# Accumulating e K Vᵀ per head in the forward of a decode block's gradient, so that the backward need not read K

## The chip, the cores and the metric

The kernel runs on one core of a Trainium2 chip. The metric is device time in microseconds (us), the median of several executions; one further execution under the profiler gives the trace.

Engines are called as in the profile: PE is TensorE's matmuls, PEld its weight loads, DVE is VectorE, ACT is ScalarE, POOL is GpSimd, SP is SyncE (here it only issues transfers).

## The reference

It is one token going through an attention block with a cache and an MLP block, with the gradient of the whole. Cut to what matters:

```python
D, F, Hq, Sk, Dh = 640, 1536, 32, 8192, 192           # one token
mod = (silu(c) @ w_mod).reshape(1, 6, 1, -1)           # sa, ca, ga, sb, cb, gb
h = layernorm(x) * (1 + ca) + sa
q = (h @ wq) as 32 heads of 192
p = softmax(q . K * Dh**-0.5)                          # K, V: (32, 8192, 192) bf16
o = p @ V
x = x + ga * (o @ wo)
h = layernorm(x) * (1 + cb) + sb
x = x + gb * MLP(h)                                    # w3, w4, tanh gelu
# outputs: x, and the gradients of x, K, V, wq, wo, w3, w4, c, w_mod
```

For one query the gradients of the attention are, for each head and with `c = do . o`:

```
dP_j = V_j . do        dS_j = p_j (dP_j - c)
dV_j = p_j do          dK_j = dS_j q          dq = sum_j dS_j K_j
```

K and V are 100.7 MB each (32 x 8192 x 192 x 2 bytes), and so are dK and dV. Nearly all the time goes into moving these four and into work over their elements. Notice that only the last of the formulas, dq, needs K in the backward. With `e_j` for the unnormalised softmax weight and Z for their sum,

```
dq = ( (sum_j e_j K_j V_j^T) do  -  c sum_j e_j K_j ) / Z
```

and the two sums over j do not depend on the backward at all.

## The kernel before

Each head's 8192 rows lie as 128 partitions times 64 rows, loaded in halves of 32 rows (6144 elements on each partition; P = 128, J = 64, JH = 32, DH = 192). Here are the parts that the change and the argument touch.

The forward of a head: dot products with K on VectorE (8 of 32 rows are summed by ScalarE), softmax, then p V on TensorE with one-column weights.

```python
def fwd_stage_a(h):
    for t in range(2):
        nc.sync.dma_start(out=K_sb, in_=K_hd[h][:, js, :])
        nc.sync.dma_start(out=V_sb, in_=V_hd[h][:, js, :])
        nc.vector.tensor_tensor(out=prod, in0=K_sb, in1=qh[:, None, :].to_broadcast([P, JH, DH]), op=ALU.mult)
        for jj in range(JACC_F):
            nc.scalar.activation(out=junk, in_=prod[:, jj, :], func=ACT.Copy, accum_out=S_h[...])
        # ... two halving adds and a reduce_sum for the other rows
def fwd_stage_b(h, S_h, V_halves):
    # ... maximum over the partitions by a transpose, exp into E_all[:, h, :]
    for j in range(J):
        nc.tensor.matmul(o_ps, lhsT=E_all[:, h, j : j + 1], rhs=V_halves[t][:, jj, :], start=(j == 0), stop=(j == J - 1))
```

The backward of a head reads V and K again. dV and dK are made one row of 192 at a time, 15 of 32 rows on ScalarE and 17 on VectorE:

```python
def bwd_stage_a(h):
    for t in range(2):
        nc.sync.dma_start(out=V_sb, in_=V_hd[h][:, js, :])
        nc.sync.dma_start(out=K_sb, in_=K_hd[h][:, js, :])
        nc.vector.tensor_tensor(out=prod, in0=V_sb, in1=doh[:, None, :].to_broadcast([P, JH, DH]), op=ALU.mult)
        # ... two halving adds and a reduce_sum into dP; dS = (dP - c) * P; dS_bf
def bwd_stage_b(h, K_halves, dS_l, dSbf_l):
    for t in range(2):
        for jj in range(JH):
            nc.tensor.matmul(dq_ps, lhsT=dS_bf[:, jj : jj + 1], rhs=K_sb[:, jj, :], start=(j == 0), stop=(j == J - 1))
        for jj in range(JH):
            if jj < JA:            # 15
                nc.scalar.activation(out=dV[:, jj, :], in_=doh, func=ACT.Copy, scale=P_all[:, h, j : j + 1])
                nc.scalar.activation(out=dK[:, jj, :], in_=qh, func=ACT.Copy, scale=dS[:, jj : jj + 1])
            else:
                nc.vector.tensor_scalar(out=dV[:, jj, :], in0=doh, scalar1=P_all[:, h, j : j + 1], scalar2=None, op0=ALU.mult)
                nc.vector.tensor_scalar(out=dK[:, jj, :], in0=qh, scalar1=dS[:, jj : jj + 1], scalar2=None, op0=ALU.mult)
        st_eng.dma_start(out=dV_hd[h][:, js, :], in_=dV)
        st_eng.dma_start(out=dK_hd[h][:, js, :], in_=dK)
```

Everything between the loops (layer norms, MLP and its gradient) works on rows of one partition, 640 or 1536 elements long, which are turned into columns by matmuls and back:

```python
def vecmat(col_bf, nk, W_sb, N, out_row, chunk=512, ...):    # a row = column^T W
    nc.tensor.matmul(ps[0:1, : hi - lo], lhsT=col_bf[:, i : i + 1], rhs=W_sb[:, i, lo:hi], ...)
def row_to_col(row_ap, ncols, out_aps, ...):
    nc.tensor.matmul(ps[:, i : i + 1], lhsT=row_ap[0:1, i * P : (i + 1) * P], rhs=one[0:1, 0:1], ...)
```

The gradient of wo is made between the loops, those of wq and w_mod after the backward, when dq of all heads is there.

## Time and profile before

The median is 1872.15 us in three runs (1871.21 to 1873.1).

| stage | from, to (us) | time | per head |
|---|---|---|---|
| start: mod, q | 0 to 58 | 58 | |
| forward of 32 heads | 58 to 606 | 548 | 16.7 from the fifth head on, 17.1 in the mean |
| middle: MLP and its gradient, do | 606 to 787 | 181 | |
| backward of 32 heads | 787 to 1757 | 970 | about 30 |
| tail: gradients of wq, w_mod, x, c | 1757 to 1871 | 114 | |

These are lines of the page of the kernel before: the busy time of each engine, the packets, and the shares of the chain of waits that ended last.

```profile
PE 767.4 (41%) x5447; PEld 571.7 (31%) x5447; DVE 1490.0 (80%) x3065; ACT 1026.4 (55%) x3391; POOL 101.3 (5%) x180
...
DMA packets 113278, 678.95 MB, mean 363 GB/s; under 512 B 53779, under 2 KB 53782, under 8 KB 63382
...
DMA 44%; DVE 38%; PE 9%; issue 5%; ACT 2%; POOL 1%; DVEq 0%; POOLq 0%; SPq 0%
```

And the table by windows, one line for each of the last four stages. Its columns are the window, its length, the busy time of PE, PEld, DVE, ACT and POOL (with their instructions), the granted clock, the DMA share and GB/s. The DMA share is the mean busy share of the core's 16 DMA engines:

```profile
58.10:606.00 547.90, 281.94 (x2263) 232.07 (x2263) 450.75 (x349) 223.27 (x1181) 2.38 (x1) 0.69 0.95 377
606.00:787.00 181.00, 104.26 (x486) 58.12 (x486) 69.29 (x139) 32.63 (x69) 19.38 (x26) 0.62 0.54 153
787.00:1757.00 970.00, 305.97 (x2342) 240.46 (x2340) 888.07 (x2509) 700.64 (x2040) 68.34 (x128) 0.63 0.99 417
1757.00:1871.00 114.00, 24.94 (x136) 11.36 (x136) 72.03 (x43) 48.41 (x66) 10.10 (x17) 0.58 0.53 212
```

Read them together. In both loops the DMA engines are full or nearly so (0.95 and 0.99), and VectorE is not far behind: 451 of 548 us in the forward, 888 of 970 in the backward. In the other two stages nothing is full: DMA 0.54 and 0.53, VectorE 38% and 63%. Those are chains of short operations that wait for one another. The chain of waits of the backward shows the DMA limit directly. It goes from one V transfer to the product that frees its buffer, to the next V transfer (start, us, what):

```profile
1203.99 26.57 DMA V_sb<-in_A_v_cache_dram
...
1230.59 3.37 DVE bprod L595
```

Three groups of VectorE (count, then busy time and the mean ns of one, then the idle time before it) price the work. A product over 6144 elements takes 3.34 to 3.36 us; a scaled row of 192 takes 0.271 us, so that 17 of them take 4.6 us:

```profile
L629 DVE TENSOR_SCALAR dK<-qs_bc,dS 128x192 bf16<-128x192 bf16 x1088 | 293.9, 271 | 0.0
...
L595 DVE TENSOR_TENSOR bprod<-V_sb,do_bc 128x6144 bf16<-128x6144 bf16 x64 | 215.1, 3361 | 61.3 <-DMA V_sb<-in_A_v_cache_dram 61.3
...
L346 DVE TENSOR_TENSOR prod<-K_sb,qs_bc 128x6144 bf16<-128x6144 bf16 x64 | 213.7, 3340 | 18.0 <-DMA K_sb<-in_A_k_cache_dram 17.9
```

### The profile page before, as it was taken

The page shows a single profiled execution, that of the slowest core. Times are in us where ns is not written, and L with a number is a line of the kernel's source. Part 1 is how long each engine was busy: PE and PEld are TensorE (multiplying, and loading weights), DVE is VectorE, ACT ScalarE, POOL GpSimd, SP SyncE. Part 2 cuts the span into 40 slices and gives each one's busy share as a digit, 9 for nine tenths or more (in the row PEclk, how much of TensorE's full clock was granted, in tenths as well). Part 3 has the DMA queues.
Part 4 walks back from the last instruction along what each step waited for, and adds up shares of the span by engine and source line. Part 5 has one row for each costly group of instructions (what it writes and reads, how often), then busy time and mean ns, then how long its engine had stood idle before and what let it go on. Part 6 is the DMA issues. An engine that isn't in the chain of part 4 may idle for free.

```text
span 1871.0 us, 18774 instructions
## 1 busy us (share of the span) xinstructions
PE 767.4 (41%) x5447; PEld 571.7 (31%) x5447; DVE 1490.0 (80%) x3065; ACT 1026.4 (55%) x3391; POOL 101.3 (5%) x180
## 2 busy tenths in 40 slices
PE   8435554555555755542322324132232313233510
PEld 5234443444444424131222213132221212222300
DVE  1668888888888254399899999999999999999485
ACT  3434444444444211295767777776777777778452
POOL 0000000000000010100000000000000000000010
PEclk8767676777677765665656666565656666566855
DMA  8799999999997426699999999999999999997944
GB/s 341 293 410 397 380 377 382 371 376 380 378 382 287 135 74 170 228 419 429 428 429 430 428 429 430 429 428 429 419 429 408 425 429 430 429 417 312 406 183 158
DMA packets 113278, 678.95 MB, mean 363 GB/s; under 512 B 53779, under 2 KB 53782, under 8 KB 63382
## 3 DMA queue, kind: packets, MB, share of 16 engines
q1 hardware_dynamic: 87590, 440.03, 59.2%
q0 software_dynamic: 25584, 237.71, 30.3%
q8 instruction: 43, 0.70, 0.1%
q14 instruction: 61, 0.50, 0.1%
HBM read 440.01 MB, written 225.91 MB: 356 GB/s over the span
## 4 chain that ended last, share of the span: by engine, by line
DMA 44%; DVE 38%; PE 9%; issue 5%; ACT 2%; POOL 1%; DVEq 0%; POOLq 0%; SPq 0%
DMA V_sb<-in_A_v_cache_dram 38%; DVE prod L346 11%; DVE bprod L595 7%; DVE S_h L355 4%; DMA K_sb<-in_A_k_cache_dram 3%; PE col_ps L188 2%; PE vm_ps L200 2%; DVE dK L629 2%; DVE dV L628 1%; PE vb_ps L121 1%; PE negm_ps L368 1%; DMA out_dram<-dK 1%; DVE dP L601 1%; DMA wmod_sb<-in_w_mod_dram 1%; ACT E_all L372 1%
## 5 line engine op out<-in xcount | busy, mean ns | idle before, releaser
L619 PE MATMUL dq_ps<-K_sb,dS_bf 128*1 128x192 bf16 x2048 | 263.8, 309 | 576.4 <-ACT dS_bf L605 576.4
L626 ACT ACTIVATE dK<-qs_bc,dS 128x192 bf16<-128x192 bf16 x960 | 355.4, 441 | 169.4 <-DMA out_dram<-dK 165.1
L619 PEld LDWEIGHTS <-dS_bf 128*1 128x1 bf16 x2048 | 211.4, 106 | 623.7 <-ACT dS_bf L605 588.2
L625 ACT ACTIVATE dV<-do_bc,P_all 128x192 bf16<-128x192 bf16 x960 | 355.4, 441 | 75.1 <-DMA out_dram<-dV 73.7
L349 ACT ACTIVATE junk<-prod 128x192 bf16<-128x192 bf16 x512 | 178.0, 348 | 215.3 <-DVE prod L346 215.3
L629 DVE TENSOR_SCALAR dK<-qs_bc,dS 128x192 bf16<-128x192 bf16 x1088 | 293.9, 271 | 0.0
L628 DVE TENSOR_SCALAR dV<-do_bc,P_all 128x192 bf16<-128x192 bf16 x1088 | 293.4, 271 | 0.1
L595 DVE TENSOR_TENSOR bprod<-V_sb,do_bc 128x6144 bf16<-128x6144 bf16 x64 | 215.1, 3361 | 61.3 <-DMA V_sb<-in_A_v_cache_dram 61.3
L379 PE MATMUL o_ps<-V_sb,E_all 128*1 128x192 bf16 x2048 | 239.6, 295 | 0.0
L346 DVE TENSOR_TENSOR prod<-K_sb,qs_bc 128x6144 bf16<-128x6144 bf16 x64 | 213.7, 3340 | 18.0 <-DMA K_sb<-in_A_k_cache_dram 17.9
L379 PEld LDWEIGHTS <-E_all 128*1 128x1 bf16 x2048 | 204.5, 102 | 28.2
L349 ACT ACTIVATION_READ_ACCUMULATOR junk<-prod 128x1 f32 x512 | 95.4, 186 | 0.0
L630 POOL DMA_DIRECT2D out_dram<-dV x64 | 34.3, 536 | 874.9 <-DVE dK L629 735.0
L375 DVE RECIPROCAL rinv_all<-tot_ps 1x1 f32<-1x1 f32 x32 | 5.0, 155 | 56.4 <-PE tot_ps L374 56.4
L631 POOL DMA_DIRECT2D out_dram<-dK x64 | 34.1, 533 | 18.2 <-DVE dK L629 17.9
L544 DVE TENSOR_SCALAR dwo_sb<-dao_bc,o_col_f 128x640 bf16<-128x640 bf16 x48 | 15.8, 393 | 24.2 <-DMA out_dram<-dwo_sb 23.1
L384 ACT ACTIVATE o_h<-o_ps,rinv_all 1x192 f32<-1x192 f32 x32 | 13.2, 411 | 37.9 <-PE o_ps L379 37.9
L121 PE MATMUL vb_ps<-woT,dao_col_bf 128*1 128x512 bf16 x60 | 23.0, 524 | 23.3 <-DMA woT<-in_A_wo_dram 23.3
L413 POOL DMA_DIRECT2D w_sb<-in_B_w_dram x1 | 0.9, 892 | 570.9 <-PE vm_ps L200 570.9
L125 ACT CAST do_row_bf<-vb_ps 1x512 bf16<-1x512 f32 x12 | 6.8, 574 | 43.6 <-PE vb_ps L121 43.6
L368 PE MATMUL negm_ps<-negm,ones_row_f 1*128 1x1 f32 x64 | 18.6, 357 | 19.4 <-ACT negm L366 19.4
L368 PEld LDWEIGHTS negm_ps<-negm,ones_row_f 1*128 1x128 f32 x64 | 15.9, 305 | 28.8 <-ACT negm L366 28.8
(893 smaller groups left out, 1259.8 us busy)
## 6 DMA issues: line engine op xcount, KB each, us to landing
K_sb<-in_A_k_cache_dram SPq DMA_DIRECT2D x128, 1536.0 KB, 14.7
V_sb<-in_A_v_cache_dram SPq DMA_DIRECT2D x128, 1536.0 KB, 15.1
out_dram<-dV POOLq DMA_DIRECT2D x64, 1536.0 KB, 14.5
out_dram<-dK POOLq DMA_DIRECT2D x64, 1536.0 KB, 21.3
wq_sb<-in_A_wq_dram SPq DMA_DIRECT2D x1, 7680.0 KB, 33.4
wo_sb<-in_A_wo_dram POOLq DMA_DIRECT2D x1, 7680.0 KB, 69.5
out_dram<-dwo_sb POOLq DMA_DIRECT2D x12, 640.0 KB, 5.0
out_dram<-stg POOLq DMA_DIRECT2D x10, 768.0 KB, 4.3
```

What stands on the lines that cost most here:

```text
L121: nc.tensor.matmul(ps[0:1, : hi - lo], lhsT=col_bf[:, i : i + 1], rhs=W_sb[:, i, lo:hi], start=(i == 0), stop=(i == nk - 1))
L346: nc.vector.tensor_tensor(out=prod, in0=K_sb, in1=qh[:, None, :].to_broadcast([P, JH, DH]), op=ALU.mult)
L349: nc.scalar.activation(out=junk, in_=prod[:, jj, :], func=ACT.Copy, accum_out=S_h[:, t * JH + jj : t * JH + jj + 1])
L355: nc.vector.reduce_sum(out=S_h[:, t * JH + JACC_F : (t + 1) * JH], in_=h2, axis=AX.X)
L368: nc.tensor.matmul(negm_ps, lhsT=ones_row_f[0:1, :], rhs=negm[0:1, 0:1], start=True, stop=True)
L379: nc.tensor.matmul(o_ps, lhsT=E_all[:, h, j : j + 1], rhs=V_halves[t][:, jj, :], start=(j == 0), stop=(j == J - 1))
L595: nc.vector.tensor_tensor(out=prod, in0=V_sb, in1=doh[:, None, :].to_broadcast([P, JH, DH]), op=ALU.mult)
L619: nc.tensor.matmul(dq_ps, lhsT=dS_bf[:, jj : jj + 1], rhs=K_sb[:, jj, :], start=(j == 0), stop=(j == J - 1))
L625: nc.scalar.activation(out=dV[:, jj, :], in_=doh, func=ACT.Copy, scale=P_all[:, h, j : j + 1])
L626: nc.scalar.activation(out=dK[:, jj, :], in_=qh, func=ACT.Copy, scale=dS[:, jj : jj + 1])
L628: nc.vector.tensor_scalar(out=dV[:, jj, :], in0=doh, scalar1=P_all[:, h, j : j + 1], scalar2=None, op0=ALU.mult)
L629: nc.vector.tensor_scalar(out=dK[:, jj, :], in0=qh, scalar1=dS[:, jj : jj + 1], scalar2=None, op0=ALU.mult)
```

## The change

The intent is to take K's second reading (101 MB) out of the backward, to take the rows of one partition out of the middle, and to leave no separate stage for the weight gradients.

- **Forward.** Each K row is scaled by its `e_j` (16 rows at a time: 10 on VectorE, 6 on ScalarE), and TensorE accumulates `(e K)ᵀ [1, V]` over the head: two matmuls with full 128-column weights for each row. V lands in pieces of two rows (768 bytes), between columns of ones that give `sum e K` and Z along with the rest. Four columns of e behind the 192 of K give o.
- **A scalar in four copies.** To multiply a vector by one scalar per row in one `tensor_tensor`, `e_j` is stored four times over. The innermost dimension of every operand then steps by one element, over four elements.
- **Backward.** It reads V alone. dK is one product over 6144 elements; of dV, 18 of 32 rows go to ScalarE one by one and 14 are one product over 2688 elements.
- **Vectors as columns.** A vector of 640 is 128 x 5, so the middle's operations have 5 or 12 elements on each partition in place of 640 or 1536 on one.
- **Weight gradients in the backward.** Each of the first 16 heads carries a sixteenth of wo and wq, the next ten a tenth of w_mod each. dq comes from the accumulated matrix: four small products with `do`.

The core of the diff, with cuts:

```diff
 # forward
-        V_sb = fv.tile([P, JH, DH], BF16, name="V_sb")
-        nc.sync.dma_start(out=V_sb, in_=V_hd[h][:, js, :])
+    def load_v(h, t):                     # VP = 388: two rows of 192 between pairs of ones
+        vb = VB[nv[0] % NVB]              # NVB = 3
+        nc.sync.dma_start(out=vb[:, :, 2 : 2 + PW], in_=V_hd[h][:, t * JH : (t + 1) * JH, :].rearrange("p (a b) d -> p a (b d)", b=2))
...
-    for j in range(J):
-        nc.tensor.matmul(o_ps, lhsT=E_all[:, h, j : j + 1], rhs=V_halves[t][:, jj, :], ...)
+    A_.activation(out=E4, in_=S_h[:, :, None].to_broadcast([P, J, 4]), func=ACT.Exp, bias=negm[:, 0:1], scale=1.0)
+    # scale_k, for 16 rows (NVA = 6 of them on ScalarE, n = 10 here):
+    V_.tensor_tensor(
+        out=ks[:, 0:n, 0:DH].rearrange("p j (a b) -> p j a b", b=4),
+        in0=kb[:, k0 : k0 + n, :].rearrange("p j (a b) -> p j a b", b=4),
+        in1=E4[:, j0 : j0 + n, None, :].to_broadcast([P, n, DH // 4, 4]), op=ALU.mult)
+    # m_quarter, for each row k:
+    T_.matmul(mp[:, o : o + DH + 2], lhsT=ks[:, k * KW : k * KW + P], rhs=rhs, ...)
+    T_.matmul(mp[:, MO + o : MO + o + DH + 2], lhsT=ks[:, k * KW + P : k * KW + 2 * P], rhs=rhs, ...)
 # backward
-        nc.sync.dma_start(out=K_sb, in_=K_hd[h][:, js, :])
-        nc.tensor.matmul(dq_ps, lhsT=dS_bf[:, jj : jj + 1], rhs=K_sb[:, jj, :], ...)
-        nc.vector.tensor_scalar(out=dV[:, jj, :], in0=doh, scalar1=P_all[:, h, j : j + 1], ...)
-        nc.vector.tensor_scalar(out=dK[:, jj, :], in0=qh, scalar1=dS[:, jj : jj + 1], ...)
+        def times(out3, vec, e4, n0_, n1_):
+            n = n1_ - n0_
+            V_.tensor_tensor(
+                out=out3[:, n0_:n1_, :].rearrange("p j (a b) -> p j a b", b=4),
+                in0=vec.rearrange("p (a b) -> p a b", b=4)[:, None, :, :].to_broadcast([P, n, DH // 4, 4]),
+                in1=e4[:, n0_:n1_, None, :].to_broadcast([P, n, DH // 4, 4]), op=ALU.mult)
...
+                v = load_v(h, t)
+                dot_half(v[...], doh, dP)          # product, three halving adds, reduce
+                V_.scalar_tensor_tensor(out=dS4, ...)
+                for jj in range(NA):               # NA = 18
+                    A_.activation(out=dV[:, jj, :], in_=doh, func=ACT.Copy, scale=Ef[...])
+                times(dV, doh, E4[:, js, :], NA, JH)
+                nc.gpsimd.dma_start(out=dV_hd[h][:, js, :], in_=dV)
+                times(dK, qh, dS4, 0, JH)
+                nc.gpsimd.dma_start(out=dK_hd[h][:, js, :], in_=dK)
+                # then prep_do(h + 1), prep_dwo(h), prep_dq(h) in heads 0 to 15; w_mod's chunks after
...
+        def outer_chunk(w, v3, rows, dst, acc, lay):       # one chunk of 384 columns of wq or w_mod
+            V_.tensor_copy(out=v_bf, in_=v3)
+            wT = transposed(...)                           # TensorE, then ScalarE
+            T_.matmul(ps[:, i : i + 1], lhsT=wT[...], rhs=v_bf[:, b : b + 1], ...)
+            V_.tensor_tensor(out=acc, in0=ps, in1=acc, op=ALU.add)
+            T_.transpose(out=tp[0:3, :], in_=v3, identity=ident_f)
+            V_.tensor_copy(out=vrow, in_=tp[0:3, :])
+            T_.matmul(bp[...], lhsT=pick(3, b), rhs=vrow[:, lo:hi], ...)
+            A_.copy(out=v_bc, in_=bp[:, 0:PW])
+            V_.tensor_scalar(out=stg[:, i, :], in0=v_bc, scalar1=rows[:, i : i + 1], ...)   # five times
+            nc.gpsimd.dma_start(out=dst, in_=stg)
```

## The prediction

> **What bounds it now.** The chain of waits is 44% DMA and 38% VectorE. In the slice table the forward (about 60 to 610 us) moves 380 GB/s with the DMA engines 97% busy; one head takes 16.7 us (two K and two V halves of 1.5 MB). The backward (780 to 1757 us) moves 426 GB/s with the DMA engines full, about 30 us per head. So both loops are DMA-bound, VectorE close behind (83% and 93% busy in the table by windows). Between them lie 170 us of one-partition vector work, and after them a 114 us tail (wq, w_mod gradients); both are chains of latencies with DMA half idle. The first K product starts only at 58 us.
>
> **What the change does.** It removes K's second read (101 MB), most of the middle and the tail, and the backward's 2048 dq matmuls. 679 MB become about 573. It adds to the forward: e*K on VectorE/ScalarE and twice the matmuls, with full 128-column weights. It replaces 17+17 small VectorE scalings per half head by one or two broadcast products.
>
> **Cost, from trace durations.** VectorE products of bf16: 6144 elements 3.36 us, 3072 1.75, 1536 0.95, so 60 ns + 0.52 ns per element. The Trainium skill ("VectorE: DVE Perf Modes", the perf-mode tier table) caps tensor_tensor at two elements per cycle, reductions at one; these durations agree. I assume that the four-copy broadcast (innermost step 1) keeps the doubled rate; no record of before shows that shape.
> - Forward, VectorE per head: two dot products of 7.6 us (3.36+1.75+0.95+0.5+0.9, plus dependency gaps), four e*K pieces of 1.1, small things 1.2: about 21 us, against 13.8 before. The forward becomes VectorE-bound: about 21.5 us per head, 690 us. DMA needs some 18 to 19 us per head (V now lands in 768-byte pieces, slower), PE 128 x 0.11 to 0.13 us = 14 to 17, ScalarE 11.
> - Start-up: 28 us instead of 58. Last head's pipeline plus middle in columns: 70 us instead of 170.
> - Backward, VectorE per half: 7.6 + 0.3 + 1.5 (14 of 32 rows of dV) + 3.3 (dK) = 12.7 us, 25.4 per head, 813 us. Weight-gradient work: about 6 us for each of 16 heads and 2 for each of 10 chunks, 110 us, plus 40 of stalls on PE/ScalarE round trips. DMA (343 MB, about 840 us) and ScalarE fall below VectorE. About 960 us.
> - Tail: 18 us.
>
> Sum: 28+690+70+960+18 = **1766 us**. So the forward loses about 140 us; start, middle, tail and backward give back about 245. The 101 MB saved pay little by themselves, because VectorE takes over as the limit.
>
> **Range** 1670 to 1890 us. Faster by over 2%: 0.70; within 2%: 0.13; slower: 0.17.
>
> **What would show it right.** VectorE over 90% busy in both loops, DMA share clearly under 1 (0.8 to 0.95), forward 21 to 22 us per head, the backward 28 to 33 us in the first 16 heads and about 26 in the last 16. Four-copy products: 1920 elements about 1.1 us, 6144 about 3.3 us. Middle under 80 us, no separate tail.
>
> **What would make it wrong.**
> 1. The four-copy broadcast runs at one element per cycle: dK 6.5 us, e*K 2.1; over 2000 us.
> 2. The maximum of a head goes through TensorE behind the last head's matmuls; if VectorE waits there, 3 to 6 us per head, 100 to 200 us.
> 3. Full weight loads not hidden behind matmuls: PE over 20 us per head and the forward PE-bound.
> 4. The V loads in 768-byte pieces run well under 380 GB/s, or block K loads in the queue: forward DMA-bound again.
> 5. Fewer dependency gaps than assumed: VectorE's bare sum is near 1570, so 1670 is possible.

## The result, and the profile after

The changed kernel is correct and takes 1665.68 us in the median (1664.51 to 1669.96, 4 runs). The ratio to before is 0.891 (95% interval 0.889 to 0.893). A ratio is the mean time of one kernel's fast runs over that of the other's of the same rounds, so it is not quite the ratio of the medians quoted. The time lies 100 us below the predicted one, just below the predicted range.

| stage (us) | before | predicted | after | after, from to | after less predicted |
|---|---|---|---|---|---|
| start | 58.1 | 28 | 17.4 | 0 to 17.4 | -11 |
| forward | 547.9 | 690 | 685.3 | 17.4 to 702.7 | -5 |
| middle | 181.0 | 70 | 72.6 | 702.7 to 775.3 | +3 |
| backward | 970.0 | 960 | 874.7 | 775.3 to 1650.0 | -85 |
| tail | 114.0 | 18 | 12.7 | 1650.0 to 1662.7 | -5 |

So the times came out near the prediction in four of the five stages: the forward pays 137 us, and start, middle and tail give 250 back. The backward was predicted to gain 10 us and gained 95.

The same lines of the page, after:

```profile
PE 666.1 (40%) x6611; PEld 582.7 (35%) x6611; DVE 1524.3 (92%) x1654; ACT 884.0 (53%) x2497; POOL 117.9 (7%) x190
...
DMA packets 347147, 574.34 MB, mean 345 GB/s; under 512 B 7438, under 2 KB 316686, under 8 KB 322478
...
DVE 64%; PE 14%; DMA 10%; issue 8%; ACT 2%; SPq 1%; POOL 0%; POOLq 0%; ACTq 0%
```

And the windows of the same four stages:

```profile
17.40:702.70 685.30, 478.23 (x4762) 443.93 (x4763) 632.12 (x583) 339.29 (x1072) 0.00 (x0) 0.81 0.93 317
702.70:775.30 72.60, 43.66 (x505) 38.66 (x503) 32.33 (x118) 27.29 (x66) 7.28 (x11) 0.62 0.62 205
775.30:1650.00 874.70, 138.97 (x1280) 96.43 (x1277) 853.47 (x921) 514.33 (x1351) 109.00 (x170) 0.50 1.02 382
1650.00:1662.70 12.70, 0.00 (x0) 0.00 (x0) 3.29 (x1) 0.00 (x0) 0.53 (x1) 0.50 0.52 217
```

The chain of waits has turned from DMA (44%, now 10%) to VectorE (38%, now 64%), and VectorE is busy for 632 of 685 us in the forward and 853 of 875 in the backward. But the DMA engines are no less full than they were: the share is 1.02 in the backward. That number contradicts the prediction, which gave 0.8 to 0.95 for both loops (the forward, 0.93, lies inside). There are three times as many packets, since V comes in 768-byte pieces, and the rate at a full share (the GB/s divided by the DMA share) has dropped from 421 to 375 GB/s (417 / 0.99 against 382 / 1.02).

What VectorE waits for in the whole backward (us in total, times, the longest):

```profile
DVE prod L270 <- DMA VB_239<-in_A_v_cache_dram: 8.2, 3, 4.1
DVE prod L270 <- DMA VB_236<-in_A_v_cache_dram: 5.6, 1, 5.6
DVE prod L270 <- DMA VB_242<-in_A_v_cache_dram: 4.5, 1, 4.5
DVE prod L270 <- ACT do_bc L607: 2.5, 1, 2.5
DVE dsc L584 <- PE acc_ps L583: 0.4, 2, 0.2
```

It waits 18.3 us for V, 2.5 us for the first `do`, and 0.4 us for TensorE. The prediction had put 40 us of round trips to TensorE and ScalarE here.

The order of VectorE's instructions shows how that comes about. Here is one half head near the end, where no weight work is left (start, us, engine, line, operation, out and in):

```profile
1524.73 3.35 DVE L270 TENSOR_TENSOR prod<-VB_239,do_bc 128x6144 bf16<-128x6144 bf16 x1
1528.00 3.35 DVE L647 TENSOR_TENSOR dK<-qs_bc,dS_12071 128x6144 bf16<-128x6144 bf16 x1
1531.27 1.75 DVE L279 TENSOR_TENSOR prod<-prod 128x3072 bf16<-128x3072 bf16 x1
1532.94 1.55 DVE L647 TENSOR_TENSOR dV<-do_bc,E_12097 128x2688 bf16<-128x2688 bf16 x1
1534.41 1.54 DVE L279 TENSOR_TENSOR prod<-prod 128x1536 bf16<-128x1536 bf16 x2
1535.98 0.95 DVE L280 TENSOR_REDUCE dP<-prod 128x32 f32<-128x768 bf16 x1
1536.97 0.35 DVE L669 SCALAR_TENSOR_TENSOR dS_12109<-dP,cpr,E_all 128x128 bf16<-128x128 f32 x1
1537.24 3.35 DVE L270 TENSOR_TENSOR prod<-VB_242,do_bc 128x6144 bf16<-128x6144 bf16 x1
```

This is not the order of the source, where dK follows its own dS and the next V product comes after dK. Here the dK of the half before stands between a V product and its first halving add, and dV between two adds. Neighbours that do not depend on each other overlap a little: dK starts at 1528.00, although the product before it ends at 1528.08. One half takes 12.51 us (1537.24 - 1524.73), and the 11 halves from 1499.71 to 1637.31 have just this mean. Sixty-four of them are 801 us, so all weight-gradient work adds 875 - 801 = 74 us, of which 18 are the waits for V.

That is what the work adds, not what it takes. Summed over the trace of the backward, the products alone keep VectorE busy for 796 us and all its other instructions (the weight work) for 92; together it is 853, so 35 us of the two lie on top of each other.

The Trainium skill ("VectorE: DVE Perf Modes", the perf-mode tier table) says that `tensor_tensor` on bf16 runs at two elements per cycle and reductions at one. The lines agree: 6144 elements in 3.35 us are 0.55 ns each, the reduction of 768 takes 0.95 us, 1.24 ns each, somewhat more than twice as much.

### The profile page after: what moved, and what is told of

It is laid out like the page before. It is cut to its first block, busy times and chain, and to the rows that moved or that the text cites. A ratio compares the mean times of both kernels' runs of the same rounds, so it can differ in the third digit from the quotient of the medians.

```text
span 1662.7 us, 18656 instructions
## 1 busy us (share of the span) xinstructions
PE 666.1 (40%) x6611; PEld 582.7 (35%) x6611; DVE 1524.3 (92%) x1654; ACT 884.0 (53%) x2497; POOL 117.9 (7%) x190
## 4 chain that ended last, share of the span: by engine, by line
DVE 64%; PE 14%; DMA 10%; issue 8%; ACT 2%; SPq 1%; POOL 0%; POOLq 0%; ACTq 0%
DVE prod L270 18%; DVE prod L279 18%; DVE dK L647 8%; PE mp L343 5%; PE mp L344 5%; DMA VB_239<-in_A_v_cache_dram 5%; DVE dV L647 5%; DVE dP L280 3%; DMA VB_236<-in_A_v_cache_dram 2%; DVE S_h L280 2%; DMA VB_242<-in_A_v_cache_dram 2%; DVE KS_258 L326 2%; DVE KS_260 L326 2%; DMA w_st<-in_A_wq_dram 1%; DVE KS_256 L326 1%
## 5 line engine op out<-in xcount | busy, mean ns | idle before, releaser
L679 ACT ACTIVATE dV<-do_bc,Ef 128x192 bf16<-128x192 bf16 x1152 | 405.9, 446 | 30.0 <-DMA out_dram<-dV 29.9
L279 DVE TENSOR_TENSOR prod<-prod 128x3072 bf16<-128x3072 bf16 (+2 forms) x384 | 415.9, 1083 | 3.9
L348 ACT COPY M_230<-mp 128x196 f32<-128x196 f32 x32 | 10.3, 323 | 171.7 <-PE mp L344 171.7
L583 PE MATMUL acc_ps<-v_bf,wqT 128*128 128x1 bf16 x390 | 14.2, 165 | 203.6 <-DVE v_bf L578 203.0
L343 PE MATMUL mp<-VB_236,KS_256 128*128 128x194 bf16 x352 | 82.9, 296 | 21.8 <-DVE KS_256 L326 21.7
L583 PEld LDWEIGHTS <-wqT 128*128 128x128 bf16 x390 | 14.5, 106 | 214.1 <-issue 214.0
L343 PE MATMUL mp<-VB_242,KS_258 128*128 128x194 bf16 x336 | 76.4, 290 | 30.5 <-DVE KS_258 L326 30.5
L343 PEld LDWEIGHTS <-KS_258 128*128 128x128 bf16 x688 | 73.3, 106 | 36.5 <-DVE KS_258 L326 34.9
L343 PE MATMUL mp<-VB_239,KS_260 128*128 128x194 bf16 x336 | 74.3, 285 | 25.5 <-DVE KS_260 L326 25.5
L343 PEld LDWEIGHTS <-KS_256 128*128 128x128 bf16 x688 | 73.9, 107 | 28.5 <-DVE KS_256 L326 26.8
L270 DVE TENSOR_TENSOR prod<-VB_239,do_bc 128x6144 bf16<-128x6144 bf16 x22 | 73.6, 3348 | 10.8 <-DMA VB_239<-in_A_v_cache_dram 8.2
L344 PE MATMUL mp<-VB_236,KS_256 128*128 128x194 bf16 x352 | 82.7, 295 | 0.6 <-ACT KS_256 L325 0.6
L343 PEld LDWEIGHTS <-KS_260 128*128 128x128 bf16 x672 | 70.3, 105 | 31.0 <-DVE KS_260 L326 29.6
L567 ACT COPY wqT<-wT_ps 128x1024 bf16<-128x1024 bf16 x26 | 26.3, 1012 | 97.7 <-PE acc_ps L583 91.5
L344 PE MATMUL mp<-VB_242,KS_258 128*128 128x194 bf16 x336 | 76.0, 287 | 0.2 <-ACT KS_258 L325 0.2
L344 PEld LDWEIGHTS <-KS_256 128*128 128x128 bf16 x688 | 75.1, 109 | 2.6 <-ACT KS_256 L325 1.0
L270 DVE TENSOR_TENSOR prod<-VB_236,do_bc 128x6144 bf16<-128x6144 bf16 x21 | 70.3, 3347 | 5.6 <-DMA VB_236<-in_A_v_cache_dram 5.6
L344 PEld LDWEIGHTS <-KS_258 128*128 128x128 bf16 x688 | 74.1, 108 | 1.8 <-ACT KS_258 L325 0.4
L270 DVE TENSOR_TENSOR prod<-VB_242,do_bc 128x6144 bf16<-128x6144 bf16 x21 | 70.3, 3347 | 4.5 <-DMA VB_242<-in_A_v_cache_dram 4.5
L344 PE MATMUL mp<-VB_239,KS_260 128*128 128x194 bf16 x336 | 73.9, 282 | 0.2 <-ACT KS_260 L325 0.2
L565 PE MATMUL wT_ps<-ident_bf,w_st 128*128 128x128 bf16 (+1 forms) x470 | 50.2, 309 | 56.5 <-ACT woT L568 38.5
L344 PEld LDWEIGHTS <-KS_260 128*128 128x128 bf16 x672 | 71.4, 106 | 1.5 <-ACT KS_260 L325 0.4
```

Source lines behind the costliest of these rows:

```text
L270: V_.tensor_tensor(out=prod.rearrange("p (a b) d -> p a b d", b=2), in0=src4, in1=vec[:, None, None, :].to_broadcast([P, JH // 2, 2, DH]), ...
L279: V_.tensor_tensor(out=prod[:, :, 0:w], in0=prod[:, :, 0:w], in1=prod[:, :, w : 2 * w], op=ALU.add)
L343: T_.matmul(mp[:, o : o + DH + 2], lhsT=ks[:, k * KW : k * KW + P], rhs=rhs, start=s, stop=e, skip_group_check=True)
L344: T_.matmul(mp[:, MO + o : MO + o + DH + 2], lhsT=ks[:, k * KW + P : k * KW + 2 * P], rhs=rhs, start=False, stop=e, skip_group_check=True)
L348: A_.copy(out=M1[:, h, :], in_=mp[:, 0:MW])
L565: T_.transpose(out=tp[lo:hi, x * P : (x + 1) * P], in_=src, identity=ident_bf)
```

## The experiments

Twelve kernels ran; the medians of before were 1873.16, 1870.96 and 1871.07 us, so chips agree within 0.2% and times can be compared across them. Several differences from the changed kernel below are 8 to 19 us, about 1%; they are used where the runs of the two kernels do not overlap and the 95% intervals of their ratios do not either. Two questions lead.

1. *Why is the backward 85 us below its sum?* The first theory is the order: the sum counts every operation and every round trip one after another, but weight work and products fill each other's gaps. The rivals are that the work itself is cheaper than costed, or that it is limited by its transfers rather than by its arithmetic.
2. *What was the removed reading of K worth?* The prediction says little, since VectorE takes over as the limit. The rival is that DMA and VectorE are both full after the change, and that each would set the time alone.

### Reading K again, for nobody

```diff
+        KR = [bk1.tile([P, JQ, DH], BF16, name=f"KR{b}") for b in range(3)]
...
                 v = load_v(h, t)
+                for q in (2 * t, 2 * t + 1):
+                    nc.sync.dma_start(out=KR[(4 * h + q) % 3], in_=K_hd[h][:, q * JQ : (q + 1) * JQ, :])
```

The accumulated matrices M1 and M2 are kept in bf16 to make room. The result stays correct.

> The backward reads K again (101 MB, nobody uses it; M kept in bf16 to make room, so dq is coarser). Theory A, as predicted: VectorE is the limit and the DMA engines have slack, so the saved bytes pay little by themselves: at most +40 us, 1706 us or less. Theory B: the DMA engines were already full in the backward (busy share 1.03 at 386 GB/s), so 101 MB cost about 101/0.386 = 260 us less some slack of the last heads: 1870 to 1925 us, with VectorE waiting for V loads or for stores to free buffers, busy under 80% in the backward.

Measured: 1907.63 us (2 runs), ratio 1.019 (1.016 to 1.023) to before, 242 us more than the changed kernel. These are VectorE's wait for V and the window of the backward:

```profile
DVE prod L270 <- DMA VB<-in_A_v_cache_dram: 231.2, 19, 17.2
```

```profile
775.30:1890.00 1114.70, 133.44 (x1234) 91.87 (x1232) 852.71 (x917) 511.02 (x1346) 107.84 (x170) 0.50 1.02 388
```

VectorE does the same 853 us of work and waits 231. The DMA share is 1.02, as without the second reading: the engines were full before it was added, so it is paid for in full. That settles the second question. The two limits stand next to each other, and with the rest of the change in place the saved K bytes are worth about 240 us. Without that part the kernel is no faster than before: 1.9% slower in these two runs, which the interval leaves unclear at 2%.

### One copy of the scalar in place of four

```diff
-                out=out3[:, n0_:n1_, :].rearrange("p j (a b) -> p j a b", b=4),
-                in0=vec.rearrange("p (a b) -> p a b", b=4)[:, None, :, :].to_broadcast([P, n, DH // 4, 4]),
-                in1=e4[:, n0_:n1_, None, :].to_broadcast([P, n, DH // 4, 4]),
+                out=out3[:, n0_:n1_, :],
+                in0=vec[:, None, :].to_broadcast([P, n, DH]),
+                in1=e4[:, n0_:n1_, 0:1].to_broadcast([P, n, DH]),
```

> dV and dK products read their per-row factor with an innermost step of 0 instead of from four adjacent copies. If the four copies are what keeps the doubled rate: 6144 elements take about 6.5 us instead of 3.35, 2688 about 2.9 instead of 1.55, so 64 x 4.4 = 283 us more: about 1945 us. Rival, the rate does not depend on that step: 3.35 us and 1666 us.

Measured: correct, 1942.72 us (2 runs), ratio 1.038 (1.034 to 1.042), 277 us more than with four copies. The groups:

```profile
L647 DVE TENSOR_TENSOR dK<-qs_bc,dS 128x6144 bf16<-128x6144 bf16 x64 | 419.0, 6547 | 0.0
L647 DVE TENSOR_TENSOR dV<-do_bc,E 128x2688 bf16<-128x2688 bf16 x64 | 188.4, 2944 | 0.0
```

They take 6.55 and 2.94 us, against 3.35 and 1.55 in the changed kernel, for the same elements. The Trainium skill ("Vector Engine (DVE) Microarchitecture Reference", section 5.1) says that the doubled rate of 16-bit operands needs an innermost step of one element, that a two-source operation with one element read again and again as an input ran at the single rate, and that a row read again and again keeps the doubled one. This pair of runs agrees with all of it, and shows that rows of four are long enough. The 64 x (3.20 + 1.40) = 294 us of longer products come back as 277 us of time.

### The weight work kept together behind its half head

The same instructions, but VectorE's are held in the order of the source: the weight work of a half head comes after the half's dK, and the next half's products after that work. (`issue_after` makes what follows come behind the given instruction.)

```diff
+        after = lambda x: tc.issue_after(x[0].ins) if x[0] is not None else nullcontext()
...
+                with after(tail):
                     v = load_v(h, t)
                     # ... the products of the half
-                times(dK, qh, dS4, 0, JH)
+                    tail[0] = times(dK, qh, dS4, 0, JH)
+                with after(tail):
                     if t == 0:
                         # ... prep_do, prep_dwo, the w_mod chunks; else prep_dq
                         # (the last tensor_scalar of each becomes tail[0])
```

> VectorE's weight-gradient instructions are kept together behind the products of their half head, not mixed with the next ones. If the round trips through TensorE and ScalarE were hidden only by the mixing (VectorE waits 0.4 us for PE in the whole backward of the changed kernel): two round trips of 1.5 to 2 us in each of 26 chunks and some gaps, +80 to +130 us, 1745 to 1795 us. Rival: the round trips themselves are short, under +20 us.

Measured: correct, 1747.84 us (1747.34 to 1750.11, 4 runs), ratio 0.934 (0.932 to 0.936), 82 us more than the changed kernel. The backward takes 961 us, from 775 to 1736. The prediction had 960. This is the last part of one head's weight work on VectorE (idle time before an instruction, and what ended it, in brackets):

```profile
1026.14 0.17 DVE L580 CAST v_bf<-dq 128x3 bf16<-128x3 f32 x1
1026.93 0.17 DVE L586 TENSOR_TENSOR dha<-acc_ps,dha 128x5 f32<-128x5 f32 x1 [0.63 <-PE acc_ps L585]
1027.57 0.28 DVE L590 CAST vrow<-bc_t 3x128 bf16<-3x128 f32 x1 [0.46 <-PE bc_t L588]
1028.92 1.24 DVE L598 TENSOR_SCALAR stg<-v_bc,ha 128x384 bf16<-128x384 bf16 x5 [1.08 <-ACT v_bc L595]
1030.08 3.35 DVE L270 TENSOR_TENSOR prod<-VB,do_bc 128x6144 bf16<-128x6144 bf16 x1
```

Each of the brackets is a round trip that VectorE sits out. In the changed kernel such instructions (here the cast into `vrow` and the five scalings into `stg`) stand among products, without a wait. This is VectorE's timeline there:

```profile
1035.99 1.75 DVE L279 TENSOR_TENSOR prod<-prod 128x3072 bf16<-128x3072 bf16 x1
1037.65 0.27 DVE L588 CAST vrow<-bc_t 3x128 bf16<-3x128 f32 x1
1037.86 0.94 DVE L279 TENSOR_TENSOR prod<-prod 128x1536 bf16<-128x1536 bf16 x1
1038.72 1.54 DVE L647 TENSOR_TENSOR dV<-do_bc,E_9482 128x2688 bf16<-128x2688 bf16 x1
1040.19 1.22 DVE L596 TENSOR_SCALAR stg<-v_bc,ha 128x384 bf16<-128x384 bf16 x5
```

The window of the backward splits the 86 us in two, and the largest of VectorE's waits in it (us in total, times, the longest) are these:

```profile
775.30:1736.00 960.70, 130.49 (x1273) 94.76 (x1270) 890.48 (x924) 514.99 (x1349) 105.17 (x171) 0.51 0.96 349
```

```profile
DVE stg L598 <- ACT v_bc L595: 24.7, 23, 1.1
DVE vrow L590 <- PE bc_t L588: 11.9, 26, 0.5
DVE dha L586 <- PE acc_ps L585: 10.1, 16, 0.6
DVE prod L270 <- ACT do_bc L609: 6.4, 1, 6.4
DVE dsc L586 <- PE acc_ps L585: 6.3, 10, 0.6
```

VectorE is idle for 70 us (960.7 - 890.5) against 21 in the changed kernel. Its busy time is also 37 us longer for nearly the same instructions (924 against 921). Neighbours that depend on each other do not overlap, as those in the late half head above do: the half's period without weight work is 12.755 us here in place of 12.51, which is 16 of the 37 over 64 halves. Most of the rest is weight work that no longer overlaps with products: products (808 us alone) and weight work (90 alone) now share 7 us, against 35. The DMA share falls to 0.96, and no wait for V is left. So the order is the answer to the first question: it is worth 82 us, nearly the whole of the 85. That the 961 us meet the 960 predicted is luck in part. The 64 halves take 816 us here (813 predicted), and the rest 144 (150), but with 59 us of waits in front of weight instructions and 6 for the first `do`, where 40 were predicted, and some 80 us of work where 110 were. So the first rival, cheaper work, holds for some 20 to 30 us of the sum, and in this order dearer stalls make up for it.

### The weight gradients' transfers without their arithmetic

The loads and stores stay, the arithmetic is dropped and a constant tile is stored. In the first version VectorE copied one column of each loaded weight tile, so that the load has a reader:

```diff
-            (all of outer_chunk but the store; prep_dq's products; prep_dwo's products)
+            V_.tensor_copy(out=acc[:, 0:1], in_=w[:, 0, 0:1])
             nc.gpsimd.dma_start(out=dst, in_=stg)
```

> Weight gradients in the backward (wq, wo, w_mod): loads and stores kept, all their arithmetic dropped (wrong values on purpose). If VectorE bounds the backward: its about 75 us of such work go, 1590 to 1605 us. If the DMA engines bound it: 1640 us or more, and VectorE waits for DMA instead. Under my prediction's 110 us of work and 40 us of stalls it would fall by 150 to about 1515.

Measured: 1676.63 us (4 runs), ratio 0.896. Its output is wrong, which doesn't matter for the time. The run was flawed: VectorE now waited 69 and 25 us for weight loads that it had never waited for before. It was mended by letting TensorE touch the tile:

```diff
-            V_.tensor_copy(out=acc[:, 0:1], in_=w[:, 0, 0:1])
+            T_.matmul(sp[:, 0:1], lhsT=w[:, 0, 0:P], rhs=w[:, 0, 0:1], start=True, stop=True)
```

> The run wg_dma_only mended: there a tiny VectorE copy of each loaded weight tile made VectorE wait 94 us for weight loads; here TensorE touches the tile instead. Loads and stores of the weight gradients kept, their arithmetic on VectorE, ScalarE and mostly TensorE dropped (wrong values on purpose). If VectorE bounds the backward: about 75 us go, 1590 to 1605 us. If the DMA engines bound it (343 MB at 390 GB/s is 880 us, the backward takes 875): 1645 us or more.

Measured: 1674.11 us (1671.56 to 1676.5, 4 runs), ratio 0.895. Dropping the arithmetic brought nothing; it even cost 8 us. The first half of the backward:

```profile
775.30:1224.00 448.70, 54.58 (x333) 35.13 (x331) 358.14 (x238) 232.59 (x627) 65.19 (x98) 0.52 1.03 380
```

VectorE had 91 us to spare in these 449, and the DMA engines none (1.03). This points to the other limit on its own. It is not clean: the order of the instructions changed too, and two of VectorE's waits, 31 and 25 us, were for matmuls that stood behind weight loads, so that most of its idle time is not a wait for V. What speaks for the DMA limit is the share.

### The weight gradients' arithmetic without their transfers

One weight tile is loaded once and used for every chunk, and only the last store of each output is made.

```diff
-            w = load_w(wq_v, t * PW)
-            outer_chunk(w, dq, ha, ...)
+            outer_chunk(wkeep, dq, ha, ..., t == NT - 1)       # stores only at the end
```

> The weight gradients' arithmetic kept, their loads and stores dropped but for the last (wrong values on purpose): about 39 MB less through the DMA engines. If VectorE bounds the backward: only its 18 us of waits for V go, 1645 to 1660 us, busy share of DMA in the backward about 0.93. If the DMA engines bound it: up to 39/0.39 = 100 us less, cut off by VectorE's 853 us of work at 1640. So both theories meet here near 1645; a time above 1660 says that DMA has no part.

Measured: 1647.58 us (1646.75 to 1649.72, 4 runs), ratio 0.881 (0.880 to 0.883), 18 us less than the changed kernel. Its output is wrong, which doesn't matter for the time. The waits for V are gone, all 18.3 us of them, and VectorE is busy for 446 of the 449 us of the first half:

```profile
775.30:1224.00 448.70, 110.70 (x968) 75.88 (x967) 446.17 (x595) 285.35 (x721) 37.03 (x64) 0.50 0.96 346
```

So with less to move the backward is VectorE's alone, and with less to compute the DMA engines stay full. The changed kernel stands 18 us above VectorE's limit.

### V in one piece per partition

In the backward nobody needs the columns of ones, so V can land in one run of 12288 bytes per partition in place of 16 pieces of 768 bytes.

```diff
-                v = load_v(h, t)
+                v = load_v_flat(h, t)        # the same buffer, without gaps
```

> V lands in one piece of 12288 bytes per partition in the backward (as in the kernel before) instead of 16 pieces of 768 bytes. If the short pieces slow the DMA engines: their busy share in the backward falls from 1.03 to about 0.95 at the same GB/s, VectorE's waits for V (18 us) vanish: 1645 to 1655 us. Rival, piece length does not matter: share stays 1.03, 1666 us.

Measured: correct, 1646.97 us (1646.26 to 1647.54, 4 runs), ratio 0.881 (0.879 to 0.882), 19 us less than the changed kernel. The window of the backward:

```profile
777.40:1633.00 855.60, 139.02 (x1280) 96.44 (x1277) 852.67 (x921) 514.89 (x1351) 109.10 (x170) 0.50 0.98 390
```

VectorE does the same 853 us of work in 856, and waits for no V. The queue that loads moved the same 347 MB in 199,658 packets in place of 322,538. A full share carries 398 GB/s (390 / 0.98), against 375 with pieces (382 / 1.02). The kernel before had 421, so the pieces explain half of the drop; what takes the other half is not shown.

### V in aligned pieces

The pieces stay, but they start at a multiple of 32 bytes: a pitch of 832 bytes and an offset of 32, in place of 776 and 4.

```diff
-    VP = PW + 4
+    VP = 416
+    VO = 14                                  # the ones start here, the row 2 elements on
```

> V's pieces stay 768 bytes but start at multiples of 32 bytes (pitch 832 instead of 776, offset 32 instead of 4), in forward and backward. If it is the odd start that slows them: forward's DMA share falls from 0.93 to 0.87 or less at 317 GB/s. If it is their length: share within 0.02 of 0.93. Time in both cases within 15 us of 1666, because VectorE is busy 92% of the forward.

Measured: correct, 1654.99 us (1651.76 to 1656.84, 4 runs), ratio 0.885 (0.883 to 0.887), 11 us less than the changed kernel. VectorE waits 12.5 us for V in place of 18.3. In the first half of the backward a full share carries 382 GB/s (393 / 1.03):

```profile
775.30:1224.00 448.70, 107.31 (x950) 73.12 (x950) 440.98 (x566) 281.03 (x710) 62.47 (x93) 0.50 1.03 393
```

The same window gives 375 for the changed kernel (386 / 1.03). The forward's share, by which the expectation meant to tell the start of the pieces from their length, came out between its two forecasts: 0.90 at 318 GB/s, from 0.93 at 317. So both seem to have a part. Some 3 to 4 of the 11 us lie before the backward.

Compare the three rates with a page. The Trainium skill ("DMA: Bandwidth & Descriptors", "Why small descriptors are slow") gives each packet about three cycles on top of one per 32 bytes; for 768 bytes an estimate from this is 27 / 24, 12.5% more time. V is 101 of about 334 MB here (382 GB/s in 874.7 us). If the rest costs what it costs at 398 GB/s, the measured 382 and 375 make V's bytes 14% dearer in aligned pieces and 20% in those at an offset of 4 bytes. (Both are estimates from the three rates: 1/382 = 0.70/398 + 0.30/x gives x = 349. The shares are known to 0.01 only, which alone moves each percentage by 2 to 4 points.) The aligned case fits the page within that. The same page's specification table gives 512 bytes as the size for the line rate; pieces of 768 bytes are above it, and carried 382 GB/s aligned and 375 at an offset of 4 bytes, against 398; the latter cost 19 us.

### Weight gradients after the loop

```diff
-                        prep_dwo(h)            # and finish_x, the w_mod chunks, prep_dq
+        for t in range(NT):                    # after the loop over heads
+            prep_dwo(t)
+            prep_dq(t)
+        finish_x()
+        for g in range(NG):
+            outer_chunk(load_w(wm_v, g * PW), ...)
```

> The weight gradients of wq, wo and w_mod after the loop over the heads instead of inside it. Inside, they cost the changed kernel about 874 - 64 x 12.5 = 74 us of backward, of which 18 are waits for V. Afterwards nothing long hides their round trips: 55 us of VectorE work, 26 chunks with about 2 us of waits and 18 us less in the loop: 1700 to 1750 us. Rival: DMA is the limit in the loop and they were in the way there, so at the end they cost no more: 1660 to 1680.

Measured: correct, 1684.72 us (1683.45 to 1685.22, 4 runs), ratio 0.901 (0.899 to 0.902). That is only 19 us more than the changed kernel; I had expected 35 to 85. The time after about 1592 us is the separate stage: 91 us, of which VectorE is busy for 60, with a DMA share of 0.68. So much of what mixing gives is given by something else as well: chunks next to each other fill each other's round trips. Mixing is worth 19 us against a dense block of chunks, and 82 against chunks that stand alone among products in the order of the source. What is expensive is a dependent chain with nothing beside it.

### More rows of e K on ScalarE

```diff
-    NVA = (3 * JQ) // 8        # 6 of 16 rows
+    NVA = 8
```

> In the forward ScalarE scales 8 of 16 rows of K by e instead of 6, VectorE 8 instead of 10 (1536 elements, about 0.95 us, instead of 1920, 1.15). If VectorE bounds the forward (busy 92%): 4 x 0.2 us x 32 heads = 26 us less, 1640 us. If the DMA engines do (share 0.93 with 768-byte pieces): less than 8 us, above 1658.

Measured: correct, 1675.17 us (1671.79 to 1676.95, 4 runs), ratio 0.895, 9 us *more* than the changed kernel. VectorE's busy time fell by 17 us (1524 to 1507), but it waits more in the forward:

```profile
DVE negm L310 <- PE mx L308: 36.1, 31, 3.3
DVE KS L326 <- PE mp L344: 18.3, 18, 1.1
```

In the changed kernel the first of these is 20.8 us and the second a few us. VectorE is busiest in the forward, but a loop from exp to e K to TensorE to the next maximum turns beside it, and with other durations the instructions came in another order, on TensorE too. Why this order costs more is open.

### Two versions made from the findings

Both take V in one piece in the backward and in aligned pieces in the forward, and 22 of 32 rows of dV on ScalarE, whose busy time in the backward is 514 of 875 us. The first takes 8 of 16 rows of e K on ScalarE, the second 10.

```diff
-        NA = (9 * JH) // 16        # 18
+        NA = 22
-    NVA = (3 * JQ) // 8            # 6
+    NVA = 8                        # second version: 10
```

> All that the runs so far favour: V in one piece per partition in the backward, V's pieces aligned to 32 bytes in the forward, ScalarE takes 22 of 32 rows of dV (18) and 8 of 16 rows of e*K (6). From v_flat's 1647: VectorE 64 x 4 x 0.1 = 26 us less in the backward if DMA (share 1.00) lets it, and 26 less in the forward: 1595 to 1615 us. If DMA holds the backward at 400 GB/s: about 1620.

> As best_a, but ScalarE takes 10 of 16 rows of e*K: VectorE another 26 us less in the forward, ScalarE 18 of about 19 us per head busy. If VectorE still bounds the forward: 1570 to 1590. If ScalarE or DMA takes over: no better than best_a.

Measured (4 runs each): 1625.57 us (1625.06 to 1628.05), ratio 0.869, and 1605.30 us (1604.83 to 1608.50), ratio 0.859 (0.857 to 0.860). Both are correct. The second beats the changed kernel by 3.6% (0.8586 / 0.8909). Its forward and backward:

```profile
17.00:685.00 668.00, 553.14 (x4792) 424.75 (x4792) 591.69 (x582) 509.40 (x1572) 0.00 (x0) 0.84 0.92 327
760.00:1590.00 830.00, 139.07 (x1284) 96.67 (x1282) 826.67 (x919) 600.66 (x1608) 105.62 (x170) 0.50 0.99 402
```

The backward is VectorE's again, 827 of 830 us. In the forward VectorE is now 76 us below the window's length and DMA stands at 0.92; neither is full, and more relief of VectorE there need not help. That 8 rows lose and 10 win is not explained, but the loss repeats: with aligned pieces the last matmul into the accumulated matrix ends at 716 us with 6 rows (the run with aligned pieces), 726 with 8 and 703 with 10. The 1626 and 1605 us of the two versions are both above what was expected of a kernel that VectorE bounds (1595 to 1615, 1570 to 1590).

## Why the prediction was right or wrong

**Right: what bounded the kernel before, and where the change pays and gains.** Both loops were DMA-bound and VectorE took over. The forward came out at 21.4 us per head (predicted 21.5) and 685 us (690), the middle at 72.6 (70). The products cost what was said: 1.15 us for 1920 elements in four copies (1.1), 3.35 for 6144 (3.3). The feared single rate did not occur, and the one-copy run shows that it was a real danger, 277 us large. The feared wait for the maximum through TensorE came to 22.6 us over the whole run in place of 100 to 200.

**Wrong, and the main miss: "Weight-gradient work: about 6 us for each of 16 heads and 2 for each of 10 chunks, 110 us, plus 40 of stalls on PE/ScalarE round trips."** The two terms sum to 150 us; the weight work added 74, of which 18 are waits for V that the sum did not have at all. So the step that failed is the laying end to end. The stalls of 40 us were not there (0.4 us for TensorE, 2.5 for the first `do`), and of the work, 92 us of VectorE's time in place of 110, 35 lie on top of the products. The other term, 813 us of products at 12.7 us a half, measured 801 at 12.51, for the same reason on a smaller scale: dependency gaps are filled by other work. The sum was made in the order of the source. Held to that order, the backward takes 961 us against the 960 predicted; free, it takes 875. The price of the products was right (12.755 us a half in that order), those of the weight work and of the stalls were not (80 and 65 us there, for 110 and 40), and only their sum met the measured time. Point 5 of the prediction named the danger, "Fewer dependency gaps than assumed", but the sum did not use it. The prediction could also have caught this in itself: it said "28 to 33 us in the first 16 heads and about 26 in the last 16", which makes 864 to 944 us and not 960. Measured were 28.5 and 26.1.

**Wrong: "DMA (343 MB, about 840 us) and ScalarE fall below VectorE."** For ScalarE that holds (514 of 875 us). The DMA share stayed at 1.02. 343 MB in 840 us are 408 GB/s, close to the 417 of the backward before, where V came in large pieces; a full share carried 375. With V in large pieces again it carried 398, so the small pieces are most of this miss and not all of it. It cost only 18 us, since VectorE's own limit lies that close.

**Wrong: "The 101 MB saved pay little by themselves, because VectorE takes over as the limit."** Reading K again costs 242 us. (No run takes this reading alone out of the kernel before. There VectorE was busy for 888 of the 970 us, so at most 82 us could have come of it with VectorE's work as it was; for that case the sentence may hold. It fails for the kernel that it was used for, where DMA was to have slack.) The reading was saved at a stage that is full with DMA, and VectorE was relieved by another part of the change at the same time. Two limits at nearly the same height each look worth little to remove while the other stands, and both parts of the change were needed.

**Small sizes.** The start took 17.4 us (28), the tail 12.7 (18): both chains shorter than costed, 16 us together.

**Open.** What sets the forward exactly: VectorE is busy for 92% of it, the DMA share is 0.93, and of its 53 idle us the wait for the maximum through TensorE is the largest part; no run separates these. Nor is it explained why moving rows to ScalarE first loses and then wins. What holds the full-share rate at 398 GB/s with V in one piece, where the kernel before had 421, is open too. In the runs without arithmetic the instruction order changed, so that they bound the DMA limit rather than measure it.

## What to carry to other kernels

When you add up the work of an engine, add the independent instructions end to end, and count the round trips of a dependent chain only where nothing else can run beside it: here the same work took 961 us in the order of the source and 875 mixed. Cost both resources of a stage after the change with the sizes of the transfers it will really make, for if both come out within a few per cent of each other, the time is set by both. And before you call a saved transfer worth little, put it back in for nobody to use: that one run gives its price beside the rest of the change.

## What the Trainium skill lacked or had wrong

- "DMA: Bandwidth & Descriptors" gives 512 bytes as the smallest transfer at line rate. Pieces of 768 bytes were still slower: 375 GB/s at a full share with them (382 when they land aligned), 398 with one piece of 12288 bytes per partition, in a mix where V is 30% of the bytes; 19 us of the kernel's time.
- The same page tells of the alignment of what a descriptor reads, not of where it lands. Moving the destination of these pieces from an offset of 4 bytes in a pitch of 776 to 32 in 832 raised the full-share rate from 375 to 382 GB/s and took 11 us off.
- The same page ("Where 436 GB/s comes from") says that for HBM to SBUF the HBM side, about 358 GB/s, binds. Taken alone that misleads; a note under its table of measurements limits the figure to both cores of a pair streaming. With one core at work the kernel before moved 417 GB/s over its 970 us of backward, reading and writing.
- "TensorE: Matmul & The Clock Gate" (LDWEIGHTS) gives a weight load P / 1.2 ns for P columns. For 128 columns that is 107 ns, and the changed kernel's 688-fold groups have means of 106 to 109 ns. But one-column loads in the kernel before also took 102 and 106 ns in the mean, 2048 of each.
- "Vector Engine (DVE) Microarchitecture Reference", section 5.1, asks for more than one element in the innermost dimension, but does not say how long the repeated rows were that it saw keep the doubled rate with two sources. Rows of four bf16 kept it (3.35 us for 6144 elements, against 6.55 with one).
- No page that I read prices what the order of instructions does to one engine: overlap between independent neighbours and hidden round trips were together 82 us here.
